# All operations and PSUM banks of an attention-plus-gating kernel in one computed list schedule with hand-placed semaphores, with pair-packed gate, row-tiled value projection and merged output tails

## The chip, the cores and the metric

The kernel runs on one core of one Trainium2 chip. Times are device microseconds of that core. "Span" is the time from the first to the last instruction of the profiled execution; the measured time is some 2 us longer. An execution counts as slow when it is over 1.5% above the fastest of the same kernel; verdicts use the fast ones. On one core the state of a single execution is not always known.

Words used below: PE is the TensorE matmul, PEld its weight load, DVE VectorE, ACT ScalarE, POOL GpSimd. SPq and POOLq are the queues on which the SP and POOL engines issue transfers. The **mode** of a matmul is the part of the array that it uses, rows times columns, as the profile prints it: `128*128` (full), `64*128` (one of two row halves), `128*64` (one of two column halves).

## The reference

Eight batches; each has eight heads of 576 rows of 64 numbers.

```python
def phi(x):                                   # for q and k
    proj = einsum('bhsd,df->bhsf', x, w_phi)  # 64 -> 128
    proj = proj - max(abs(proj), axis=-1)
    return concat([exp(proj), exp(-proj)])    # 256 features
kv  = einsum('bhsf,bhsd->bhfd', phi(k), v)
z   = sum(phi(k), axis=2)
x   = einsum('bhsf,bhfd->bhsd', phi(q), kv) / (einsum('bhsf,bhf->bhs', phi(q), z) + 1e-6)
# x is seen as (8, 576, 512)
gate = sigmoid(causal convolution of x over rows, 5 taps, one weight per channel and tap)
out  = (gate * (x @ w_val)) @ w_out
```

## The kernel before

Per batch it does the K and Q features (PK, PQA: matmul, maximum on DVE, exponentials on ACT), the scaling of v by the maxima (VT, on POOL), the sums KVPS, the numerators and denominators NUM, the transposed x (XT), gate and value (GATE, VAL), and the output. K and Q reach PE transposed: a casting load from DRAM to DRAM on POOL's queue, then a transposing DMA on SP's queue.

```python
    def load_rows(st, src, name, parts):
        b = st.b
        T = qtp.tile([P, H * HALF], BF16, name=name)
        rows = src[b].rearrange("h s d -> h (s d)").rearrange("h (i x) -> i h x", x=256)
        hn = H // parts
        for c in range(parts):
            R = dram.tile([hn * 2 * P, 2 * D], BF16, name=f"{name}R{parts}")
            nc.gpsimd.dma_start(
                R[:, :].rearrange("(h i y) x -> i h (y x)", h=hn, y=2), rows[0:P, c * hn:(c + 1) * hn, :],
            )
            nc.sync.dma_start_transpose(T[:, c * hn * 2 * P:(c + 1) * hn * 2 * P], R[:, :])
        R = dram.tile([H * NT, 2 * D], BF16, name=f"{name}Rt")
        nc.gpsimd.dma_start(
            R[:, :].rearrange("(h i y) x -> i h (y x)", h=H, y=2), rows[P:HALF // 2, :, :],
        )
        nc.sync.dma_start_transpose(T[:, TAIL:H * HALF], R[:, :])
        return T
```

The gate is a convolution, done as ten 128 x 128 matmuls with diagonal weights for each quarter of the channels; the value projection is eight full matmuls:

```python
    def unit_valgate(st, jt):
        XT = st.XT
        GATE = ps2.tile([P, 2, 512], FP32, name="GATE", tag="b")
        for tap in range(5):
            for par in range(2):
                t = par + tap - 4
                i0 = PAD + t // 2
                nc.tensor.matmul(
                    GATE[:, par, 0:HALF], DIAG[:, jt, tap, :], XT[:, jt, t % 2, i0:i0 + HALF],
                    start=(tap == 0), stop=(tap == 4),
                )
        GS = mlp.tile([P, 2, HALF], BF16, name="GS")
        nc.scalar.activation(GS[:, :, :], GATE[:, :, 0:HALF], AF.Tanh)
        VAL = ps2.tile([P, 2, 512], FP32, name="VAL", tag="b")
        for dt in range(4):
            for par in range(2):
                nc.tensor.matmul(
                    VAL[:, par, 0:HALF], WVAL[:, dt, jt * P:(jt + 1) * P],
                    XT[:, dt, par, PAD:PAD + HALF], start=(dt == 0), stop=(dt == 3),
                )
        with nc.allow_low_precision("bf16 gv"):
            nc.vector.scalar_tensor_tensor(
                out=st.GV[jt][:, :, :], in0=GS[:, :, :], scalar=1.0, in1=VAL[:, :, 0:HALF],
                op0=ALU.add, op1=ALU.mult,
            )
```

The order is made by hand: two lists of units are interleaved by weights, and all PSUM tiles are pairs of banks from one pool of four.

```python
... (unit_k, unit_qmax, unit_vscale, unit_qproj, unit_kv, unit_num, unit_xt, unit_out: one function per unit)

    def merge(ua, ub):
        ta, tb = sum(w for w, _ in ua) or 1.0, sum(w for w, _ in ub) or 1.0
        ia = ib = 0
        fa = fb = 0.0
        while ia < len(ua) or ib < len(ub):
            if ib >= len(ub) or (ia < len(ua) and fa <= fb):
                fa += ua[ia][0] / ta
                ua[ia][1]()
                ia += 1
            else:
                fb += ub[ib][0] / tb
                ub[ib][1]()
                ib += 1

    for i in range(B + 1):
        if i + 1 < B:
            load_qk(states[i + 1])
            load_v(states[i + 1])
        if i < B:
            alloc_A(states[i])
            alloc_B(states[i])
        merge(
            units_features(states[i]) if i < B else [],
            units_num(states[i - 1], (2, 3, 4)) + units_mlp(states[i - 1]) if i > 0 else [],
        )
        if i == 0:
            late_constants()
        if i < B:
            merge(units_qproj(states[i]), units_kv(states[i]) + units_num(states[i], (0, 1)))
```

## Time and profile before

| | before |
|---|---|
| measured time, median of 2 | 394.84 us (393.51 to 396.16) |
| span of the profiled execution | 391.9 us |
| PE, DVE, ACT busy | 66%, 44%, 48% of the span |
| one batch in the steady stretch | 40.8 us |

The page of the kernel before: the span, the busy time, and three rows of 40 equal slices (9.8 us each), in which each digit is tenths of busy time, or of full clock.

```profile
span 391.9 us, 6901 instructions
PE 257.9 (66%) x2876; PEld 163.0 (42%) x2876; DVE 171.6 (44%) x253; ACT 186.5 (48%) x261; POOL 142.4 (36%) x207
...
PE   0023387950018895889597958796769856995794
...
PEclk9999998995559898889978996899698969897898
DMA  9994799999997217500742055201600210012003
```

No engine is near its limit, and the row of PE shows a gap of three to four slices after the first fifth. The table of busy time by stretches (start and end in us, length, then each engine's busy us and instructions, the granted PE clock, DMA share, GB/s) gives one steady batch, the gap, and a short stretch inside a batch:

```profile
130.37:170.36 39.99, 31.83 (x359) 20.18 (x360) 21.11 (x31) 22.37 (x30) 13.64 (x20) 0.88 0.36 90
...
79.00:119.00 40.00, 8.65 (x84) 5.21 (x84) 2.76 (x5) 8.40 (x13) 15.03 (x21) 0.62 1.29 193
154.00:160.00 6.00, 5.45 (x61) 3.34 (x60) 0.92 (x2) 1.94 (x2) 1.39 (x2) 0.50 0.92 246
```

In the gap PE works 8.65 of 40 us. The list of waits (who waited for whom: total us, times, longest) names its cause:

```profile
PE KVPS L326 <- ACT OUTs L426: 32.1, 8, 30.7
ACT OUTs L426 <- DMA out_dram<-OUTs: 29.9, 2, 28.2
```

and the timeline of SP's queue in the same stretch shows the store of OUTs behind transposes:

```profile
76.59 8.67 SPq L79 DMA_TRANSPOSE KT<-KTR_1073  x1
...
96.07 8.47 SPq L79 DMA_TRANSPOSE KT<-KTR_1615  x1
104.63 1.00 SPq L432 DMA_DIRECT2D out_dram<-OUTs  x2
```

Each of the large transposes (there are three in this stretch) held the queue for over 8 us (8.67, 8.04 and 8.47), so the store was issued only at 104.6 us, ACT could not reuse its buffer, and PE waited for ACT. In the steady stretch the loss is of another kind: in-order waits along one batch's chain, of which PE's longest, 3.13 us, is for POOL's scaling of v. It comes back at 193.9, 234.6 and 275.5 us, once a batch. Behind it the granted PE clock is 0.50 (the last line of the table above, 154 to 160 us). It is also at half (0.51) from 129.4 to 132.9 us, after 3.5 us in which PE was busy for 1.42. The timeline of PE of before shows both (start, length, instruction, idle time before it and what ended that):

```profile
130.32 2.56 PE L394 MATMUL GATE<-XT,DIAG 128*128 128x288 bf16 x10
...
153.41 0.59 PE L332 MATMUL KVPS<-VTt_1103,KTIL 128*128 128x260 bf16 x2 [3.13 <-POOL VTt_1103 L268]
```

The ten matmuls took 2.56 us; the three groups of ten after them, at full clock, 1.41 each in the same view. (The 1.34 of the prediction is the same length in the view of the critical chain.)

### The profile page before, as it was taken

The page shows a single profiled execution, that of the slowest core. Times are in us where ns is not written, and L with a number is a line of the kernel's source. Part 1 is how long each engine was busy: PE and PEld are TensorE (multiplying, and loading weights), DVE is VectorE, ACT ScalarE, POOL GpSimd, SP SyncE. Part 2 cuts the span into 40 slices and gives each one's busy share as a digit, 9 for nine tenths or more (in the row PEclk, how much of TensorE's full clock was granted, in tenths as well). Part 3 has the DMA queues.
Part 4 walks back from the last instruction along what each step waited for, and adds up shares of the span by engine and source line. Part 5 has one row for each costly group of instructions (what it writes and reads, how often), then busy time and mean ns, then how long its engine had stood idle before and what let it go on. Part 6 is the DMA issues. An engine that isn't in the chain of part 4 may idle for free.

```text
span 391.9 us, 6901 instructions
## 1 busy us (share of the span) xinstructions
PE 257.9 (66%) x2876; PEld 163.0 (42%) x2876; DVE 171.6 (44%) x253; ACT 186.5 (48%) x261; POOL 142.4 (36%) x207
## 2 busy tenths in 40 slices
PE   0023387950018895889597958796769856995794
PEld 0022264620015552655254624562446434643571
DVE  1128046720006672567146723764195517560620
ACT  1117944450027364735564475547355636474522
POOL 8102959786000328022800471045304440426000
PEclk9999998995559898889978996899698969897898
DMA  9994799999997217500742055201600210012003
GB/s 188 172 203 103 124 211 143 187 179 183 184 234 138 46 30 208 122 7 2 204 113 48 2 142 162 63 1 56 188 2 2 72 50 2 2 45 77 2 0 120
DMA packets 85320, 39.31 MB, mean 100 GB/s; under 512 B 44709, under 2 KB 80677, under 8 KB 85290
## 3 DMA queue, kind: packets, MB, share of 16 engines
q1 hardware_dynamic: 65088, 28.32, 31.3%
q0 software_dynamic: 20032, 10.49, 20.1%
q8 instruction: 22, 0.36, 0.4%
q10 hardware_dynamic: 170, 0.08, 0.1%
q14 instruction: 8, 0.07, 0.1%
HBM read 30.48 MB, written 18.87 MB: 126 GB/s over the span
## 4 chain that ended last, share of the span: by engine, by line
PE 38%; DVE 18%; POOL 16%; DMA 10%; SPq 9%; issue 7%; ACT 1%; POOLq 0%; DVEq 0%; ACTq 0%
PE GATE L394 13%; PE VAL L403 9%; DVE XN L361 7%; SPq L79 5%; DMA QTRt<-in_q_dram 4%; DVE MK L214 4%; PE KVPS L326 4%; DMA out_dram<-OUTs 3%; PE KVPS L332 3%; PE PQ L280 3%; DVE XT L380 2%; PE PQ L285 2%; DMA KTR_96<-in_k_dram 2%; SPq L84 2%; SPq L103 2%
## 5 line engine op out<-in xcount | busy, mean ns | idle before, releaser
L219 ACT ACTIVATE KTIL<-PK 128x1024 bf16<-128x1024 f32 (+1 forms) x80 | 70.7, 940 | 72.3 <-DVE MK L214 72.3
L290 ACT ACTIVATE QTIL<-PQ 128x1024 bf16<-128x1024 f32 x64 | 61.6, 1023 | 52.8 <-PE PQ L285 52.8
L245 POOL TENSOR_SCALAR MK<-MK 128x16 f32<-128x16 f32 (+1 forms) x24 | 5.9, 245 | 166.4 <-DVE MK L214 161.0
L338 DVE CAST KVSB<-KVPS 128x520 bf16<-128x520 f32 x16 | 11.2, 700 | 109.9 <-PE KVPS L332 109.9
L394 PE MATMUL GATE<-XT,DIAG 128*128 128x288 bf16 x320 | 51.1, 312 | 1.5 <-DVE XT L382 1.5
L326 PEld LDWEIGHTS <-KTIL 128*128 128x128 bf16 x512 | 28.0, 120 | 50.3 <-issue 45.2
L214 DVE TENSOR_REDUCE MK<-PK 128x8 f32<-128x1024 f32 (+1 forms) x40 | 44.4, 1111 | 9.2 <-PE PK L196 9.0
L403 PE MATMUL VAL<-XT,WVAL 128*128 128x288 bf16 x256 | 42.0, 312 | 0.0
L420 PE MATMUL OUTp<-WOUT,GV 128*128 128x512 bf16 (+1 forms) x160 | 38.5, 380 | 4.0 <-DVE MQB_144 L228 2.3
L399 ACT ACTIVATE GS<-GATE 128x576 bf16<-128x576 f32 x32 | 20.9, 652 | 38.5 <-PE GATE L394 38.5
L394 PEld LDWEIGHTS <-DIAG 128*128 128x128 bf16 x320 | 31.5, 104 | 13.7 <-issue 0.7
L426 ACT ACTIVATE OUTs<-OUTp 128x1024 f32<-128x1024 f32 (+1 forms) x24 | 21.3, 889 | 32.7 <-DMA out_dram<-OUTs 29.9
L408 DVE SCALAR_TENSOR_TENSOR GV<-GS,VAL 128x576 bf16<-128x576 bf16 x32 | 24.1, 752 | 21.2 <-PE VAL L403 21.2
L228 DVE TENSOR_REDUCE MQB_142<-PQA 128x8 bf16<-128x1024 f32 (+1 forms) x20 | 22.2, 1112 | 22.5 <-PE PQA L196 22.5
L403 PEld LDWEIGHTS <-WVAL 128*128 128x128 bf16 x256 | 27.5, 107 | 9.8
L228 DVE TENSOR_REDUCE MQB_144<-PQA 128x8 bf16<-128x1024 f32 (+1 forms) x20 | 22.3, 1113 | 19.6 <-PE PQA L196 19.6
L196 PE MATMUL PK<-W_127,KT 64*128 64x128 bf16 x288 | 16.7, 232 | 19.4 <-DMA KT<-KTR_93 16.7
L375 PE MATMUL XTP<-ident_bf,XN 128*128 128x128 bf16 (+1 forms) x160 | 15.1, 217 | 21.2 <-DVE XN L361 20.8
L361 DVE TENSOR_TENSOR XN<-NUM,RCP 128x512 bf16<-128x512 f32 (+1 forms) x40 | 26.9, 688 | 0.9
L420 PEld LDWEIGHTS <-GV 128*128 128x128 bf16 (+1 forms) x160 | 14.7, 99 | 19.9 <-issue 4.3
L326 PE MATMUL KVPS<-VT_559,KTIL 128*128 128x65 bf16 x32 | 2.2, 219 | 31.1 <-ACT OUTs L426 30.9
L196 PE MATMUL PQA<-W_127,QT 64*128 64x128 bf16 x288 | 15.9, 229 | 9.5 <-DMA QT<-QTR_103 9.0
(226 smaller groups left out, 375.5 us busy)
## 6 DMA issues: line engine op xcount, KB each, us to landing
VN<-in_v_dram SPq DMA_DIRECT2D x16, 512.0 KB, 5.4
out_dram<-OUTs SPq DMA_DIRECT2D x24, 256.0 KB, 2.9
out_dram<-OUTs SPq DMA_DIRECT2D x8, 192.0 KB, 4.3
out_dram<-OUTs SPq DMA_DIRECT2D x8, 128.0 KB, 4.0
KTRt<-in_k_dram POOLq DMA_DIRECT2D x8, 64.0 KB, 11.0
QTRt<-in_q_dram POOLq DMA_DIRECT2D x8, 64.0 KB, 14.5
KTR_165<-in_k_dram POOLq DMA_DIRECT2D x1, 512.0 KB, 11.6
QTR_172<-in_q_dram POOLq DMA_DIRECT2D x1, 512.0 KB, 14.8
```

The source lines that it names most:

```text
L196: nc.tensor.matmul(PS[:, par, x, :], T[ROWS[par], c0:c0 + P], W2[ROWS[par], :], start=True, stop=True,)
L214: nc.vector.tensor_reduce(st.MK[:, 0, s0:s0 + 2 * n].rearrange("p (t x) -> p t x", t=2), PK[:, :, 0:n, :], AX.X, ALU.max, apply_absolute_v ...
L219: nc.scalar.activation(st.KTIL[:, sgn, s0:s0 + 2 * n, :].rearrange("p (t x) f -> p t x f", t=2), PK[:, :, 0:n, :], AF.Exp, scale=1.0 - 2.0 ...
L228: nc.vector.tensor_reduce(st.MQb[:, :].rearrange("p (t s) -> p t s", t=2)[:, :, 4 * u:4 * u + n], PQ[:, :, 0:n, :], AX.X, ALU.max, apply_a ...
L290: nc.scalar.activation(st.QTIL[:, sgn, u, :, :, :], PQ[:, :, :, :], AF.Exp, scale=1.0 - 2.0 * sgn,)
L326: nc.tensor.matmul(KVPS[:, sgn, x * E1:(x + 1) * E1], st.KTIL[:, sgn, s, :], st.VT[sgn][:, s, :], start=(x == 0 and jp == 0), stop=False, ...
L361: nc.vector.tensor_tensor(XN[0:m, :, :].rearrange("p (g x) d -> p g x d", g=2), NUMv[:, :, :, 0:D], RCP[0:m, :, :].unsqueeze(3).to_broadca ...
L394: nc.tensor.matmul(GATE[:, par, 0:HALF], DIAG[:, jt, tap, :], XT[:, jt, t % 2, i0:i0 + HALF], start=(tap == 0), stop=(tap == 4),)
L403: nc.tensor.matmul(VAL[:, par, 0:HALF], WVAL[:, dt, jt * P:(jt + 1) * P], XT[:, dt, par, PAD:PAD + HALF], start=(dt == 0), stop=(dt == 3),)
L408: nc.vector.scalar_tensor_tensor(out=st.GV[jt][:, :, :], in0=GS[:, :, :], scalar=1.0, in1=VAL[:, :, 0:HALF], op0=ALU.add, op1=ALU.mult,)
L420: nc.tensor.matmul(OUTp[0:m, n, :], st.GV[jt][:, :, :].rearrange("p t i -> p (t i)")[:, P * c:P * c + m], WOUT[:, jt, :], start=(jt == 0), ...
L426: nc.scalar.activation(OUTs[0:m, 0:len(cs), :], OUTp[0:m, 0:len(cs), :], AF.Copy)
```

## The change

The intent is to run all engines close to their limits at once. The whole kernel becomes a list of units with a priority, dependencies and a cost; a list scheduler, run when the kernel is built, hands out engines and PSUM banks one by one in the model's time, and its order is emitted with semaphores placed by hand. Besides:
- batch 0's K and Q come by plain loads and are transposed on PE; batches 1 and 2 are loaded at once, at the start;
- GATE: x is kept so that both rows of a pair lie on the partitions, and 12 matmuls of 128 x 64 (six pairs of column halves) do the five taps;
- VAL: 16 matmuls of 64 x 128, in pairs of row halves;
- the row tiles of the Q projection subtract the maxima without a masked copy;
- the last 64 rows of two batches share one output unit; half the padding in the tail of v is gone; single PSUM banks are used where one is enough.

The core of the diff (lines of "..." are cuts):

```diff
--- before.py
+++ after.py
 ...
+DVE_E, DVE_I, DVE_L = 1.0417e-3, 0.065, 0.09
+ACT_E, ACT_I, ACT_L = 0.8333e-3, 0.055, 0.12
+POOL_E, POOL_I, POOL_L = 1.93e-3, 0.06, 0.06
+PE_L = 0.19
+WAKE = 0.045
+DMA_L = 2.0
 ...
+CFG = dict(
+    period=19.0,
+    limit=dict(
+        K=1, QA=1, QF=3, KV=1, NUM=2, XT=2, MQ=1, GATE=1, VAL=1, OUT=2, T0=3,
+    ),
+    off=dict(
+        cast=-28.24, v=-6.0, DG=8.07, K=0.0, Kd=4.34, QA=1.0, QAd=4.0, EK=2.83, VT=1.85, MQ=15.13,
+        QF=19.55, QFd=3.59, KV=21.26, KVd=3.55, NUM=27.88, NUMd=3.0, XT=1.6, GATE=41.98, GATEd=3.0,
+        OUT=55.38, OUTd=1.94, store=0.5,
+    ),
+)
 ...
+    def schedule(self, limit):
 ... (event loop: at each time, each free engine)
 ...
+                    best = None
+                    for o in ready[e]:
+                        if best is not None and (o.prio, o.seq) >= (best.prio, best.seq):
+                            continue
+                        if o.rel > t + 1e-9:
+                            continue
+                        if any(self._from(x, h, e) > t + 1e-9 for x, h in o.deps):
+                            continue
+                        ps = o.ps
+                        if ps is not None and not o.new:
+                            if any(self._from(x, False, e) > t + 1e-9 for x in ps.users):
+                                continue
+                        elif ps is not None:
+                            if live.get(ps.cls, 0) >= limit.get(ps.cls, 9):
+                                continue
+                            if self._place(ps.nb, bank_free, t) is None:
+                                continue
+                        best = o
+                    if best is None:
+                        continue
+                    o = best
+                    again = True
+                    left -= 1
+                    for f in o.opts:
+                        ready[f].remove(o)
+                    o.eng, o.t0 = e, t
+                    o.t1, o.t2 = t + o.occ[e], t + o.vis[e]
+                    if o.dma is not None:
+                        o.t2 = 1e9
+                        heapq.heappush(pend, (o.t1 + 0.6, o.seq, o))
+                        heapq.heappush(times, o.t1 + 0.6)
+                    free[e] = o.t1
 ...
+    def emit(self, tc, nc):
 ... (keeps the planned order; drops waits that an earlier wait implies)
 ...
+                for k, n in need.items():
+                    E.wait_ge(sems[k], n)
+                    for kk, nn in snap[(k, n)].items():
+                        if kn.get(kk, 0) < nn:
+                            kn[kk] = nn
+                out = o.fn(E, None if o.ps is None else o.ps.at)
+                if o.dma is not None:
+                    if o.used or o.key[0] == "out":
+                        s = sem(o.key)
+                        for i in out:
+                            i.then_inc(s, 16)
+                        count[o.key] += 16 * len(out)
+                        o.mark = (o.key, count[o.key])
+                elif o.used:
+                    out[-1].then_inc(sems[o.eng], 1)
+                    count[o.eng] += 1
 ...
+def build(pl, cfg, nc=None, m=None):
 ... (constants)
 ...
+    const("WVa", "POOL", 0.8, lambda E, b: [E.dma_start(
+        m.WV[0:D, :, :], m.w_val.rearrange("(h c) j -> c h j", c=D))], -195, w=["WVa"], dma=3.1, key=("WVa",))
+    const("WVb", "SP", 0.6, lambda E, b: [E.dma_start(m.WV[D:P, :, :], m.WV[0:D, :, :])],
+          -194, r=["WVa"], w=["WVb"], dma=1.5, key=("WVb",))
+    const("WO", "POOL", 0.8, lambda E, b: [E.dma_start(
+        m.WO[:, :, :], m.w_out.rearrange("(jt p) o -> p jt o", p=P))], -194, w=["WO"], dma=3.1, key=("WO",))
 ...
+        if b == 0:
+            for g in range(2):
+                for xi, X in enumerate(("KT", "QT")):
+                    src = (m.k, m.q)[xi][0].rearrange("h s d -> (h s d)").rearrange("(c p x) -> p c x", p=P, x=P)
+                    pl.fresh(("XF", xi, g))
+                    pl.op("xf", "SP", 0.6, lambda E, b_, xi=xi, g=g, src=src: [E.dma_start(
+                        m.XF[:, 18 * xi + 9 * g:18 * xi + 9 * g + 9, :], src[:, 9 * g:9 * g + 9, :])],
+                        -300 + 2 * g + xi, w=[("XF", xi, g)], dma=1.95, key=("XF", xi, g))
+            for g in range(2):
+                for xi, X in enumerate(("KT", "QT")):
+                    for j in range(3):
+                        ps = Banks(1, "T0")
+                        c = 18 * xi + 9 * g + 3 * j
+                        pl.op("T0", "PE", 0.75, lambda E, at, c=c: [E.transpose(
+                            m.PS[:, at, P * y:P * y + P], m.XF[:, c + y, :], m.ident_f[:, :]) for y in range(3)],
+                            -100 + 10 * g + 5 * xi + j, r=[("XF", xi, g), "ident_f"], w=[], ps=ps, new=True)
+                        dst = 1152 * g + 384 * j
+                        pl.op("T0c", ("DVE", "ACT"), {"DVE": dve(384), "ACT": act(384)},
+                              lambda E, at, X=X, dst=dst: [cp(E, m.T[X][0][:, dst:dst + 384], m.PS[:, at, 0:384])],
+                              -99 + 10 * g + 5 * xi + j, w=[(X, 0, g)], ps=ps)
+        else:
+            for g in range(2):
+                for xi, X in enumerate(("KT", "QT")):
+                    src = (m.k, m.q)[xi][b].rearrange("h s d -> (h s d)").rearrange("(c p x) -> c p x", c=2, x=1024)
+                    rk = ("R", xi, g, s)
+                    pl.fresh(rk)
+                    pl.op("cast", "POOL", 0.75, lambda E, at, src=src, xi=xi, g=g: [E.dma_start(
+                        m.R[xi][g][s].rearrange("(p y) x -> p (y x)", y=8), src[g])],
+                        -205 + (10 * b if b > 1 else 0) + 2 * g + xi, w=[rk], dma=1.55,
+                        rel=max(0.0, t0 + off["cast"]), key=("R", xi, g, s))
+                    pl.op("tr", "SP", 1.6, lambda E, at, X=X, xi=xi, g=g: [E.dma_start_transpose(
+                        m.T[X][s][:, 1152 * g:1152 * g + 1152], m.R[xi][g][s][:, :])],
+                        -205 + 10 * b + 2 * g + xi, r=[rk], w=[(X, s, g)], dma=1.8, key=(X, s, g))
 ...
 ... (K and Q features, Q projection, KV, NUM; the whole of batch b in units with a priority)
 ...
+    def mlp(b):
+        s = b % 2
+        t0 = T * b
+        XT = m.XT[s]
+        rx = [("XT", s, y) for y in range(3)] + [("XT0", s)]
+        for jt in range(4):
+            pr = t0 + off["GATE"] + off["GATEd"] * jt
+            gs = ("GS", (4 * b + jt) % 3)
+            pl.fresh(gs, ("GV", s, jt))
+            GS = m.GS[gs[1]]
+            ps = Banks(2, "GATE")
+
+            def mm(E, at, jt=jt):
+                return [E.matmul(
+                    m.PS[ROWS[hh], at + p, 0:HALF], m.DG[:, 2 * jt + hh, 3 * p + dl, :],
+                    XT[:, 2 * jt + hh, dl:dl + HALF], start=(dl == 0), stop=(dl == 2), skip_group_check=True)
+                    for p in range(2) for dl in range(3) for hh in range(2)]
+
+            pl.op("GATE", "PE", 0.76, mm, pr, r=rx + ["DG"], ps=ps, new=True, vis=0.76 + PE_L)
+            pl.op("TANH", "ACT", act(576), lambda E, at, GS=GS: [E.activation(
+                GS[:, :, :], m.PS[:, at:at + 2, 0:HALF], AF.Tanh, scale=0.5)], pr, w=[gs], ps=ps)
+            ps = Banks(2, "VAL")
+
+            def mm(E, at, jt=jt):
+                return [E.matmul(
+                    m.PS[:, at + p, 0:HALF], m.WV[ROWS[p], h, P * jt:P * jt + P], XT[ROWS[p], h, PAD:PAD + HALF],
+                    start=(h == 0), stop=(h == H - 1), skip_group_check=True) for h in range(H) for p in range(2)]
+
+            pl.op("VAL", "PE", 1.0, mm, pr + 0.3, r=rx + ["WVa", "WVb"], ps=ps, new=True, vis=1.0 + PE_L)
+            pl.op("GV", "DVE", dve(576), lambda E, at, jt=jt, GS=GS: [E.scalar_tensor_tensor(
+                out=m.GV[jt][:, s, :, :], in0=GS[:, :, :], scalar=1.0, in1=m.PS[:, at:at + 2, 0:HALF],
+                op0=ALU.add, op1=ALU.mult)], pr + 0.3, r=[gs], w=[("GV", s, jt)], ps=ps)
 ...
 ... (outs: units c = 0..3 for every batch; c = 4, for odd batches, is the tail of two batches)
+            if c < 4:
+                p, j = c % 2, c // 2
+
+                def mm(E, at, p=p, j=j):
+                    return [E.matmul(m.PS[:, at, :], m.GV[jt][:, s, p, P * j:P * j + P], m.WO[:, jt, :],
+                                     start=(jt == 0), stop=(jt == 3)) for jt in range(4)]
+
+                rd = [("GV", s, jt) for jt in range(4)]
+            else:
+                def mm(E, at):
+                    return [E.matmul(m.PS[NT * (2 * y + p):NT * (2 * y + p) + NT, at, :],
+                                     m.GV[jt][:, y, p, 2 * P:HALF], m.WO[:, jt, :], start=(jt == 0), stop=(jt == 3),
+                                     skip_group_check=True)
+                            for jt in range(4) for y in range(2) for p in range(2)]
+
+                rd = [("GV", y, jt) for jt in range(4) for y in range(2)]
+            pl.op("OUT", "PE", 0.88, mm, pr, r=rd + ["WO"], ps=ps, new=True, vis=0.88 + PE_L)
+            pl.op("OUTc", ("ACT", "DVE"), {"ACT": act(512), "DVE": dve(512)},
 ...
 ... (the old body, pools and merge() are removed)
 ...
+    pl = Plan()
+    build(pl, CFG, nc, m)
+    pl.schedule(CFG["limit"])
+    with nc.allow_low_precision("bf16 operands"):
+        pl.emit(tc, nc)
```

## The prediction

> **What bounds it now.** No engine. In the table of busy time by stretches, one steady batch (from its first GATE matmul to the next batch's, 130.4 to 372.7 us) takes about 40.8 us; PE is busy 32 of it, DVE 21, ACT 22, POOL 13.6, and the DMA share is 0.1 to 0.36. The time is in-order waiting: in the chain of waits, each batch goes Kmax, OUT issue, POOL scaling of v (5.8 us), KVPS, normalisation, GATE/VAL. While PE waits 3.1 us for the POOL tail of v, DVE idles 7 us and the granted clock falls to 0.50 (154 to 160 us); the next ten GATE matmuls take 2.56 us instead of 1.34. [...] There are two one-off losses: first PE work at 16.7 us and first GATE at 64 us (transposed loads), and a stall from 79 to 119 us, PE busy 9 of 40, where a store of OUTs sits on the SP queue behind transposes of 8 to 9 us each (list of waits: 28.2 us ACT on that store, 30.7 us PE on ACT). It costs some 25 us.
>
> **Work after the change, per batch**, from measured durations (1024-wide exp 0.94 us back to back; 1024-wide max 1.13; 512-wide DVE 0.6; 512-wide POOL 1.04; 288-column matmul 0.122; 512-column 0.215; 65-column about 0.03):
> - PE: features 2.6, Q projection 2.1, KV 2.3, NUM 2.2, transposes 1.1, GATE 3.0 (was 4.9: six column-tiled pairs for ten), VAL 4.0 (same: row pairs), OUT 4.0 (was 4.3): about 21.3 us warm, against 25.
> - DVE 19, ACT 19, plus 2.4 of output copies that either may take: about 20.3 each.
> - POOL 12.5 (v tail halved) plus 3 of issue. DMA the same bytes, 4.7 MB, in longer pieces: my estimate 20 us, from transposes of 512 KB in 4 us [...].
> Row pairs are seen in this trace: two 64-row 512-column matmuls advance together at 0.22 us a pair. Column pairs are not[...].
>
> **Critical path.** Removed work is only some 4 us of PE a batch. The gain is overlap: three to four batches interleaved, single banks handed out one by one, so the period falls from 40.8 to near the fullest engine. Floors are 20 to 21 on PE, ACT, DVE and DMA at once; I expect 85 to 92% packing: period 23 to 25 us. The 79-119 stall should go. The first batch comes by plain loads and PE transposes: first K matmul at 7 to 9 us, first GATE near 45.
> Sum: PE does little before 45 us (15 of its 170 us); 155 us at 90% is 172; tail 9; about 226, plus about 3 from span to measured time: **230 us**, range **213 to 252**.
> Chances: faster by over 2% 0.97, within 2% 0.02, slower 0.01.
>
> **Signs.** PE busy above 75% of the span, DVE and ACT about 70%, granted clock near 1.0 after the ramp; GATE groups of 12 in about 0.76 us (1.4 if column pairs don't overlap); no wait over 5 us after the ramp; GATE starts of successive batches 22 to 26 us apart; DMA share 0.7 to 1.
>
> **What would make it wrong.** The order is fixed by a cost table: where loads land later than planned (DMA is nearly full, the SP queue is in order), every engine waits in its order: 27 to 30 us a batch, 250 to 270. Column tiles that don't overlap add 3 us a batch. [...] The other way, 95% packing gives about 215.

Four passages that rested on no trace are cut from it: what was said to lower the clock, a figure for column pairs, a figure for loads of v, and what a change of tiling mode may do. The sum came to 45 + 172 + 9 = 226 us of span, 230 us in measured time, and no term of it is cut. Two figures under it were not shown when they were put. GATE's 3.0 us a batch is an estimate: 24 pairs at the measured 0.122 us of one 288-column matmul, if column pairs advance together. The 20 us of DMA a batch, one of the floors but no term of the sum, is an estimate too: in the trace of before, six of the eleven transposes of 512 KB landed in 4.0 to 4.6 us (the longest in 17.0), and loads of v of 512 KB in 4.0 to 12.3 us, 5.4 in the median. That the clock was 0.50 and ten GATE matmuls took 2.56 us is measured.

## The result, and the profile after

| | before | after |
|---|---|---|
| measured time, median | 394.84 us | 258.81 us (258.60, 259.01) |
| ratio of the fast runs | | 0.6547 (95% interval 0.6484 to 0.661) |
| span | 391.9 us | 256.8 us |
| PE, DVE, ACT busy | 66%, 44%, 48% | 81%, 71%, 68% |

Ratios here and below are the mean time of one kernel's fast runs over that of the other's from the same rounds, so they are not quite the ratio of the medians quoted. The time fell by 34 to 35%, but it lies above the range of 213 to 252 us.

The page after, the same lines:

```profile
span 256.8 us, 8459 instructions
PE 206.9 (81%) x3693; PEld 144.7 (56%) x3708; DVE 181.5 (71%) x277; ACT 174.6 (68%) x240; POOL 119.1 (46%) x203
...
PE   0260838487968999899899999998998999999960
...
PEclk9999977897999999999999999999999999999997
DMA  6999999999535999789999993960170013103041
```

The gap is gone and so are the long waits of PE; but the first quarter of the span is still thin. Busy time by stretches (columns as before), from the first GATE to the end of PE's work, cut at the three merged output tails and so two batches to a line in the middle:

```profile
62.00:115.40 53.40, 48.04 (x902) 32.89 (x909) 44.52 (x65) 43.78 (x60) 28.66 (x49) 0.99 0.87 166
115.40:165.20 49.80, 47.60 (x910) 32.89 (x914) 42.63 (x64) 43.15 (x61) 26.75 (x45) 1.00 0.92 196
165.20:214.80 49.60, 47.15 (x911) 33.16 (x918) 43.27 (x64) 42.96 (x61) 23.50 (x39) 1.00 0.29 90
214.80:249.00 34.20, 32.60 (x497) 20.96 (x495) 19.17 (x33) 13.13 (x20) 4.45 (x7) 1.00 0.19 67
sum 187.00, PE 175.40 PEld 119.90 DVE 149.59 ACT 143.02 POOL 83.36; mean PE 43.85 PEld 29.97 DVE 37.40 ACT 35.76 POOL 20.84
```

PE is busy 175.4 of 187.0 us there (94%), at full clock: after the first GATE this kernel is bound by PE. One batch takes 24.8 us (49.6 / 2), inside the predicted 23 to 25. The predicted sum of three terms, beside what came of each:

| term | predicted | measured |
|---|---|---|
| ramp, to the first GATE | 45 us | 62.0 us |
| body, from there to the end of PE's work | 155 us of PE work at 90%, 172 us | 175.4 us of PE work at 94%, 187.0 us |
| tail | 9 us | 7.8 us |
| span | 226 us | 256.8 us |

So two terms of about equal size are missing: 17 us in the ramp and 15 us in the body.

**A clue for the body.** The timeline of PE after, in a dense stretch. Here the start of one group to the start of the next is read, for the length in the second column runs past the start of the next group (1.16 us in the first pair below, 1.09 from start to start):

```profile
181.67 1.16 PE L787 MATMUL PS<-XT,WV 64*128 64x288 bf16 x16
182.76 0.62 PE L720 MATMUL PS<-ident_bf,XN 128*128 128x128 bf16 x8
...
198.78 1.17 PE L787 MATMUL PS<-XT,WV 64*128 64x288 bf16 x16
199.79 0.38 PE L612 MATMUL PS<-QT,W 64*128 64x512 bf16 x2
```

The same VAL group (16 matmuls, mode 64*128) takes 1.09 us when the next group is in another mode (first pair), and 1.01 us when the next group is in its own (second pair). It is so for every kind of group that was followed by both. Between 115.4 and 214.8 us (four batches) the medians in the trace are, from start to start:

| group | next in the same mode | next in another mode | difference |
|---|---|---|---|
| K features, 8 matmuls of 64*128 | 0.235 us | 0.328 us | 0.093 us |
| end of KV, 2 of 128*128 | 0.117 us | 0.208 us | 0.091 us |
| NUM, 16 of 128*128 | 0.498 us | 0.590 us | 0.092 us |
| VAL, 16 of 64*128 | 0.996 us | 1.094 us | 0.098 us |
| GATE, 12 of 128*64 | never | 0.860 us | |

There are 104 such changes in these four batches, 26 a batch, and 191 from the first GATE to the end. At some 0.095 us each that is 18 us. The plan's cost table has 1.0 us for VAL and 0.76 for GATE: right for the work, with nothing for a change. (15 of the kernel's 3,708 matmuls, all of OUT, are missing from this trace. In e10_later, with the same order of PE and none missing, PE is busy 177.2 of 187.8 us after the first GATE, again 94%.)

**A clue for the ramp.** List of waits after, the line for PE on a transfer, and SP's queue from the start:

```profile
PE PS L428 <- DMA QTIL<-in_k_dram: 12.7, 2, 6.6
```

```profile
0.94 0.47 SPq L420 DMA_DIRECT2D QTIL<-in_k_dram  x1
1.47 0.61 SPq L420 DMA_DIRECT2D QTIL<-in_q_dram  x1
2.13 1.57 SPq L420 DMA_DIRECT2D QTIL<-in_k_dram  x1
3.74 9.52 SPq L420 DMA_DIRECT2D QTIL<-in_q_dram  x1
13.30 12.21 SPq L449 DMA_DIRECT2D VN<-in_v_dram  x2
```

(QTIL is where batch 0's plain loads are put for a while.) The issue of the fourth plain load began at 3.7 us and held the queue for 9.5 us; the four landed at 6.0, 16.2, 26.3 and 28.2 us. In that time POOL's queue had eight casting loads (batches 1 and 2) and the two weight loads under way, issued between 1.5 and 8.5 us. The trace's records of DMA packets from 2 to 26 us:

| what | packets | bytes in one | mean time of one | share of the 16 engines |
|---|---|---|---|---|
| casting loads, POOL's queue | 128 | 18,432 | 1,377 ns | 0.46 |
| weights, POOL's queue | 1,024 | 1,024 | 96 ns | 0.26 |
| plain loads of K and Q, SP's queue | 3,940 | 512 | 31 ns | 0.32 |

So the loads that the ramp waits for got a third of the DMA engines.

### The profile page after: what moved, and what is told of

Its sections match the earlier page's. It is cut to its first block, busy times and chain, and to the rows that moved or that the text cites. A ratio compares the mean times of both kernels' runs of the same rounds, so it can differ in the third digit from the quotient of the medians.

```text
span 256.8 us, 8459 instructions
## 1 busy us (share of the span) xinstructions
PE 206.9 (81%) x3693; PEld 144.7 (56%) x3708; DVE 181.5 (71%) x277; ACT 174.6 (68%) x240; POOL 119.1 (46%) x203
## 3 DMA queue, kind: packets, MB, share of 16 engines
q0 software_dynamic: 1952, 9.31, 20.2%
## 4 chain that ended last, share of the span: by engine, by line
PE 59%; DVE 16%; ACT 11%; DMA 9%; issue 2%; SPq 0%; DVEq 0%
PE PS L787 11%; PE PS L813 10%; DMA QTIL<-in_k_dram 9%; PE PS L776 9%; PE PS L665 7%; ACT QTIL L625 6%; DVE MQb L586 5%; PE PS L701 4%; ACT KTIL L500 3%; DVE MK L495 3%; PE PS L612 3%; PE PS L720 2%; PE PS L490 2%; PE PS L618 2%; DVE GV L792 2%
## 5 line engine op out<-in xcount | busy, mean ns | idle before, releaser
L537 POOL TENSOR_TENSOR VT<-VN,EK 128x512 bf16<-128x512 f32 x64 | 65.7, 1045 | 18.8 <-ACT EK L528 18.7
L625 ACT ACTIVATE QTIL<-PS 128x1024 bf16<-128x1024 f32 x64 | 61.9, 1036 | 12.6 <-PE PS L618 12.6
L500 ACT ACTIVATE KTIL<-PS 128x1024 bf16<-128x1024 f32 x64 | 62.5, 1032 | 6.4 <-PE PS L490 4.3
L586 DVE TENSOR_REDUCE MQb<-PS 128x8 bf16<-128x1024 f32 (+1 forms) x40 | 44.1, 1113 | 3.1 <-PE PS L574 2.6
L495 DVE TENSOR_REDUCE MK<-PS 128x8 f32<-128x1024 f32 x32 | 39.0, 1219 | 4.6 <-PE PS L490 2.7
L792 DVE SCALAR_TENSOR_TENSOR GV<-GS,PS 128x576 bf16<-128x576 bf16 x32 | 24.1, 753 | 18.8 <-PE PS L787 14.6
L787 PE MATMUL PS<-XT,WV 64*128 64x288 bf16 x512 | 37.1, 283 | 0.1
L776 PE MATMUL PS<-XT,DG 128*64 128x288 bf16 x384 | 30.1, 292 | 2.4 <-ACT QTIL L625 1.4
L813 PE MATMUL PS<-WO,GV 128*128 128x512 bf16 x113 | 28.3, 379 | 2.9 <-DVE GV L792 1.1
L787 PEld LDWEIGHTS PS<-XT,WV 64*128 64x128 bf16 x512 | 22.9, 94 | 8.8 <-issue 1.6
L665 PE MATMUL PS<-VT,KTIL 128*128 128x65 bf16 x512 | 22.6, 202 | 2.2 <-ACT QTIL L625 1.3
L665 PEld LDWEIGHTS PS<-VT,KTIL 128*128 128x128 bf16 x512 | 20.2, 103 | 5.1 <-issue 4.3
L428 PE MATMUL PS<-ident_f,QTIL 128*128 128x128 f32 x36 | 8.7, 425 | 14.2 <-DMA QTIL<-in_k_dram 12.7
```

The lines of the kernel that those rows point to most:

```text
L495: pl.op("Kmax", "DVE", dve(1024), lambda E, at, u=u: [E.tensor_reduce(MK[:, 0, 8 * u:8 * u + 8].rearrange("p (t x) -> p t x", t=2), m.PS[: ...
L500: pl.op("Kexp", "ACT", act(1024), lambda E, at, u=u, g=g: [E.activation(KTIL[:, g, u, :, :, :], m.PS[:, at:at + 2, :].rearrange("p t (x f) ...
L537: pl.op("VT", "POOL", pool(512), lambda E, at, u=u, hh=hh, a=a, g=g, EK=EK: [E.tensor_tensor(m.VT[s][:, g, u, :, :, 0:D], m.VN[s][:, 4 * h ...
L586: pl.op("Qmax", "DVE", dve(256 * nx), lambda E, at, u=u, nx=nx: [E.tensor_reduce(MQb[:, :].rearrange("p (t s) -> p t s", t=2)[:, :, 4 * u: ...
L625: pl.op("Qexp", "ACT", act(1024), lambda E, at, u=u, g=g: [E.activation(m.QTIL[s][:, g, u, :, :, :], m.PS[:, at:at + 2, :].rearrange("p t ...
L665: res.append(E.matmul(m.PS[:, at + sg, x * E1:(x + 1) * E1], m.KTIL[s][:, sg, 2 * g + a, par, x, :], m.VT[s][:, sg, 2 * g + a, par, x, :], ...
```

## The experiments

Twelve runs; each has runs of the kernel before on the same chip. Unless said otherwise each is the changed kernel with one edit, gave the right result, and lists four executions. The medians quoted take in all four, slow ones too; the ratios are of the fast ones alone.

### a0_after: the changed kernel again

Expected:

> The changed kernel unchanged, as the base for the other runs of this call. Both theories: 257 to 260 us, first GATE matmul near 62 us, and 24.8 us from one batch to the next in the steady stretch.

Measured: 259.41 us (258.45 to 259.61), ratio to before 0.6581. First GATE at 61.5 us; from the second to the third merged output tail (two batches) 49.5 us. It is the base for what follows: ramp 61.5, body 188.2 (to the end of PE's work), span 257.5 us.

### Changes of mode, added and paid for: e2_switch and e3_same

A one-column matmul in the middle of KV, NUM and GATE groups, once in another mode, once in the group's own. For GATE:

```diff
-                return [E.matmul(m.PS[ROWS[hh], at + p, 0:HALF], m.DG[...], XT[...], ...)
-                    for p in range(2) for dl in range(3) for hh in range(2)]
+                for p in range(2):
+                    if p == 1:   # e2_switch: 64 rows, 128 columns
+                        res.append(E.matmul(m.PS[:, at + p, 0:1], m.W2[ROWS[0], :], m.W2[ROWS[0], 0:1], ...))
+                                 # e3_same: 128 rows, 64 columns
+                        res.append(E.matmul(m.PS[ROWS[0], at + p, 0:1], m.ident_bf[:, 0:D], m.ident_bf[:, 0:1], ...))
+                    res += [... the six matmuls of this p, as before]
```

> One extra one-column matmul with 64 rows in the middle of each KV group, and of each four-head NUM and GATE group (80 in all, 160 more changes of the tiling mode); what it writes is overwritten by the next matmul, so the result stays right. Order and all else as in the changed kernel. Theory (each change of tiling mode costs PE about 0.095 us that the plan leaves out, and PE is the limit in the steady stretch): 160 x 0.095 = 15 us of PE time, of which 11 to 16 us is seen beyond the run with the same extra matmuls without a change of mode; 270 to 280 us. Rival (PE has slack in the steady stretch, which is paced by late loads or by DVE and ACT): within 4 us of that run.

> The same 80 extra one-column matmuls in the mode of the group that they stand in: the control for the run before. Theory: 80 x 0.03 to 0.06 us, so 1 to 5 us slower than the changed kernel. Rival: under 1 us slower.

Measured: e2_switch 273.82 us (272.87 to 274.20), ratio 0.6949; e3_same 260.39 us (260.20 to 260.89), ratio 0.6613. The extra matmuls alone cost 0.98 us over a0_after, on the border between theory and rival of e3_same; the 160 extra changes cost 13.4 us more, as expected. Not all of it is in the body: the first GATE comes 2.9 us later in e2_switch (14 of the changes lie before it, and the mean clock there was 0.85 against 0.91). After the first GATE, 146 extra changes made PE's busy time 12.1 us longer, 0.083 us each, and the kernel 10.0 us, 0.069 us each, since PE's idle time fell by 2.0 us. The timeline of PE in e2_switch around one GATE group:

```profile
180.06 0.56 PE L787 MATMUL PS<-XT,DG 128*64 128x288 bf16 x6 [0.47 <-DVE GV L804]
180.55 0.17 PE L786 MATMUL PS<-W 64*128 64x1 bf16 x1
180.65 0.56 PE L787 MATMUL PS<-XT,DG 128*64 128x288 bf16 x6
```

and in e3_same:

```profile
169.25 0.56 PE L787 MATMUL PS<-XT,DG 128*64 128x288 bf16 x6
169.65 0.17 PE L786 MATMUL PS<-ident_bf 128*64 128x1 bf16 x1
169.65 0.56 PE L787 MATMUL PS<-XT,DG 128*64 128x288 bf16 x6
```

From the first half of GATE to the second is 0.59 us with two changes and 0.40 without: 0.095 us a change. That changes cost PE time, and that most of this PE time is the kernel's time, is shown.

### Loads taken out of the body: e5_noload

```diff
+    gone = {o for o in pl.order if o.name in ("cast", "tr", "v", "vt") and o.seq >= pl.second}
+    pl.order = [o for o in pl.order if o not in gone]   # no loads from batch 2 on; and no waits on them
```

> Wrong result on purpose: from batch 2 on nothing is loaded; K, Q and v of batches 0 and 1 are used again, and every other instruction and its order is the same. Theory (in the steady stretch PE is the limit, with its changes of mode): the two batches between the second and the third merged output tail still take 48.4 to 50 us (49.6 in the changed kernel); the time falls only in the ramp, to 250 to 258. Rival (late loads pace the steady stretch): that interval falls under 47 us and the time under 247.

Measured: 251.62 us (251.53 to 252.07), ratio 0.6377; wrong result. The two batches between the second and the third tail took 49.5 us, exactly as with the loads, and from the first GATE to the end of PE's work it took 188.0 us (a0_after 188.2). Late loads don't pace the body: that rival fell. Of the 7.8 us that it was faster, 5.9 came from the ramp: the fourth plain load landed at 22.7 us instead of 28.1, and the first GATE started at 55.5 us instead of 61.5. Another 1.5 us came from the tail after PE's last matmul (6.3 us instead of 7.8).

### The plan told of the cost: e6_cost

```diff
+MODE = dict(K="row", QF="row", QA="row", VAL="row", Kt="row32", NUMt="col", XTt="col", GATE="col")
+TURN, KEEP = 0.095, 0.0
...
-                    o.t1, o.t2 = t + o.occ[e], t + o.vis[e]
+                    turn = TURN if e == "PE" and MODE.get(o.name, "full") != mode else 0.0
+                    o.t1, o.t2 = t + o.occ[e] + turn, t + o.vis[e] + turn
```

> The plan is told the cost of a change of tiling mode (0.095 us of PE when the next PE unit is in another mode) and draws up its order with that; nothing else differs. Theory (PE work is what it is; the plan's order already fits): within 3 us of the changed kernel, so 256 to 262 us. Rival (the body is long because the order was drawn up for a faster PE than there is): 3 to 8 us faster, 251 to 256 us.

Measured: 264.07, 268.62, 260.58 and 268.41 us; two of the four were slow. In the profiled execution (fast) the first GATE was at 63.1 us and the body took 191.3 us, with 194 changes of mode instead of 191 and 15.4 us of idle PE instead of 11.6. The rival (a better-informed order is faster by 3 to 8 us) fell; of the two fast executions one (260.58) lay in the expected 256 to 262 and one above it. In this run, knowing the cost didn't help: the priorities left as many changes as before. Why its executions spread by 8 us was not followed up.

### Holding back the loads of the ramp: e1_hold, e4_hold2, e7_hold3

Three attempts at the ramp, with the order of PE, ACT and DVE kept. First, all ten transfers on POOL's queue wait for the plain loads:

```diff
+    held = [o for o in pl.order if o.name in ("WVa", "WO") or o.name == "cast" and o.seq < pl.third]
+    last = [o for o in pl.order if o.name == "xf"][-1]
+    for o in held:
+        o.deps.append((last, True))
```

> The eight casting loads of batches 1 and 2 and the two weight loads wait until the last of the four plain loads of batch 0 has landed; every other order is the same. Theory (the first loads share the DMA engines with twelve other transfers): the last of the four plain loads lands at 13 to 16 us instead of 28, the first GATE starts at 49 to 54 us instead of 62, and the time falls by 8 to 12 us, to 247 to 251. Rival (the ramp is long because the chain of work of one batch is long and PE runs at half clock there): the loads land earlier but the first GATE moves by less than 3 us and the time by less than 3 us.

(The text says twelve transfers in its theory, and so does the next; there are ten.) Measured: 254.45 us (253.29 to 257.55, the last one slow), ratio 0.6451. (The half clock of the rival, here and in the three expectations like it below, is in the traces: in the ramp of the changed kernel it was 0.50 from 35.6 to 42.3, 49.2 to 52.5 and 59.5 to 62.8 us, and 1.00 up to 35.5 us.) The plain loads landed at 5.8, 8.1, 10.0 and 12.0 us, better than expected, but the first GATE started at 58.0 us and the time fell by 5 us: between the theory and the rival. The gain was given back to a new wait. PE's fixed order puts batch 1's K before the rest of batch 0, and batch 1's first two transposes, now beside batch 2's casts and the weights, took 22.6 and 22.3 us from issue to landing, and PE waited 4.2 us for the first.

Second, batch 2's casts are moved behind batch 0's scaling of v as well:

> As the run that held twelve loads back, but the four casting loads of batch 2 stand after batch 0's scaling of v on the POOL queue, just ahead of batch 3's first one, so that they no longer run beside batch 1's transposes; batch 1's casts and the two weight loads follow batch 0's plain loads as before. Theory (that run gave its gain back because batch 1's transposes, beside casts and weights, took 22 us instead of 4 to 7, and PE's fixed order puts batch 1's K ahead of batch 0's remaining work): batch 1's first transpose lands by 26 us instead of 39, the first GATE starts at 50 to 54 us, and the time is 246 to 251. Rival (from there on the ramp is the chain of work and the halved clock): first GATE at 57 to 59 us and 253 to 255 us, as in that run.

Measured: 269.25, 250.87, 251.28 and 269.32 us: two fast and two slow executions, and the profile fell in a slow one. The two fast ones lie where the theory put them (246 to 251, or just above); the ratio of the fast ones is 0.6361. The slow profile says how the collision looks, though it may not explain a difference between kernels: from 38 to 56 us the casts' packets of 18,432 bytes took 3,498 ns on average (1,377 in the table above) and the transposes' packets of 256 bytes 198 ns (28 in the changed kernel from 44 to 60 us). The medians did not move (1,376 and 18 ns), so some packets took very long, not all of them a little longer. The question needed another edit.

Third, one after the other, by waits: the weights wait for batch 1's third transpose, batch 2's casts for the fourth:

> The loads of the ramp one after the other, every other order kept: batch 1's casts wait for batch 0's plain loads, the two weight loads for batch 1's third transpose, batch 2's casts for batch 1's fourth transpose. Theory (in the ramp the casting loads, whose packets of 18,432 bytes hold a DMA engine for 1.4 to 3.5 us each, starve the plain loads and the transposes on the other queue, whose packets have 256 to 1,024 bytes): transposes of batch 1 land within 4 to 7 us each, first GATE at 50 to 54 us, all four executions within 1% of each other, 247 to 252 us. Rival (the ramp's length is the chain of work and the halved clock; which load runs first only shuffles it): first GATE at 57 to 61 us, 253 to 258 us.

Measured: 256.41 us (255.40 to 257.83), ratio 0.6504, first GATE at 59.1 us: a miss, in the rival's range. Batch 1's first three transposes (0.29 MB each), with few other transfers beside them, did land 3.5 to 6.5 us after issue. The list of waits shows why this doesn't speak for the rival:

```profile
PE PS L665 <- POOL VT L543: 8.3, 1, 8.3
POOL R L441 <- DMA QT<-R: 7.9, 1, 7.9
```

POOL issues the casts and also scales v, in order. While it waited 7.9 us for the transpose before it could issue a load, batch 1's v stood behind, and PE waited 8.3 us for that (L665 is KV). The edit had put a wait for a transfer in front of work.

### Loads that are not needed yet stand behind: e10_later

```diff
     held = [... the four casts of batch 1, WVa, WO ...]          # wait for batch 0's plain loads
+    late = [o for o in pl.order if o.name == "cast" and pl.second <= o.seq < pl.third]   # batch 2
+    next_ = [o for o in pl.order if o.name == "cast" and o.seq > pl.third][:2]           # batch 3
+    for o in late:
+        o.deps.append((turned, True))          # batch 1's fourth transpose
+    # both are put behind batch 1's first scaling of v on POOL
```

> As the run whose executions spread from 251 to 269 us, but the loads of batches 2 and 3 that are not yet needed (six casts) stand behind batch 1's first scaling of v on POOL, and batch 2's casts wait for batch 1's fourth transpose, so that POOL is not blocked and no cast runs beside batch 1's transposes. PE, ACT and DVE keep their order. Theory (the ramp is as long as the DMA engines need for what stands ahead of batch 0's GATE, and loads that are needed later were in front of it): first GATE at 49 to 54 us, 247 to 252 us, executions within 1.5% of each other. Rival (chain of work and halved clock): first GATE at 57 us or later, 254 us or more.

Measured: 249.26 us (248.53, 248.57, 249.95; and one slow, 253.58), ratio 0.6336. In a fast profile the plain loads landed at 5.7, 8.3, 9.9 and 11.9 us, and the first GATE started at 51.2 us instead of 61.5. SP's queue, to be read beside the one above, and the first GATE:

```profile
4.17 1.87 SPq L420 DMA_DIRECT2D QTIL<-in_q_dram  x1
6.08 2.98 SPq L449 DMA_DIRECT2D VN<-in_v_dram  x2
...
16.61 2.10 SPq L445 DMA_TRANSPOSE KT<-R  x1
...
51.18 1.00 PE L776 MATMUL PS<-XT,DG 128*64 128x288 bf16 x10
```

The body was left as it was: 187.8 us (a0_after 188.2). So 10.3 us of the ramp were transfers standing in front of what was needed first: the casts of batch 1 and the weights in front of batch 0, and the casts of batch 2 in front of batch 1; the rival, that the chain of work sets the ramp, fell for that part. The spread among executions was 2%, not within the 1.5% expected.

### Is it the bytes or the packets? e8_short

```diff
-    src = (m.k, m.q)[xi][b].rearrange("h s d -> (h s d)").rearrange("(c p x) -> c p x", c=2, x=1024)
+    src = (m.k, m.q)[xi][b].rearrange("h s d -> (h s d)").rearrange("(c a p x) -> c p a x", c=2, a=8, x=256)
-    m.R[xi][g][s].rearrange("(p y) x -> p (y x)", y=8), src[g]
+    m.R[xi][g][s].rearrange("(a p y) x -> p a (y x)", a=8, y=2), src[g]
```

> The changed kernel with one edit: the casting loads run through the same bytes in pieces of 256 numbers (512 bytes written, 1 KB read) rather than in one run of 8 rows, so that their packets are short, as in the kernel before. Nothing is held back. Theory (long packets of the cast queue starve the other queue): in the ramp the fourth plain load lands earlier than 28 us, at 18 to 24, although all the same bytes are under way; the time may go either way, since the casts themselves get slower: 252 to 264 us. Rival (the plain loads are late because of the bytes beside them, whatever their packets): the fourth plain load lands at 27 to 30 us.

Measured: 258.65 us (257.51 to 259.27 fast, one slow at 263.81), ratio 0.6536. With the same bytes under way, the fourth plain load landed at 20.2 us instead of 28.1 and the third at 14.0 instead of 26.2. The page's line for POOL's queue, after and in e8_short, shows the edit: the same megabytes in twelve times the packets.

```profile
q0 software_dynamic: 1952, 9.31, 20.2%
```

```profile
q0 software_dynamic: 23008, 9.33, 29.8%
```

From 2 to 26 us the casts' packets had 512 bytes and took 59 ns, and SP's queue got a share of 0.54 of the DMA engines for its plain loads of K, Q and v. With long packets SP's queue had had 0.32 of the engines in that stretch (the table above). So the rival (the bytes beside them, whatever their packets; 27 to 30 us) fell; how an engine shares its time among queues is not in the records. (The short casts also took POOL longer to issue, until 12.0 us instead of 9.0, which may be a small part of it.) But the casts then cost more engine time (29.8% of the span for 20.2%) and batch 1's transposes landed 12 to 14 us after issue. The first GATE came at 58.3 us, 3 us earlier than in a0_after, but the body took 192.8 us, and the time was not clearly different.

### Fewer changes of mode: e11_order and e9_fewer

The order is drawn up anew: the plan knows the 0.095 us, prefers a unit in the mode at hand when it is at most 1.6 us less urgent, and its offsets and limits were searched again under that model. By trace, 171 changes of mode in all instead of 217, and 141 instead of 191 after the first GATE.

```diff
+TURN, KEEP = 0.095, 1.585
-                        if best is not None and (o.prio, o.seq) >= (best.prio, best.seq):
+                        key = o.prio + (KEEP if e == "PE" and MODE.get(o.name, "full") != mode else 0.0)
+                        if best is not None and (key, o.seq) >= (best_key, best.seq):
 ... (CFG: new offsets and limits)
```

e11_order is this alone, with the loads as they were; e9_fewer has it together with the waits of e7_hold3 (the place of batch 2's casts follows a slightly wider rule).

> Only the new order (the one of 163 changes of mode among PE's units instead of 204), with the loads of the changed kernel left as they are. Theory (changes of mode are PE time, and PE is the limit after the ramp): 41 x 0.095 = 4 us less than the changed kernel after the first GATE, whatever the ramp does; from first GATE to last matmul 181 to 186 us instead of 187 to 188, in all 252 to 258 us. Rival (the new order gains only through the ramp): 187 us or more from the first GATE to the last matmul.

> The run above with the loads one after the other, and an order drawn up anew: the plan is told the 0.095 us of a change of mode, prefers a PE unit in the mode at hand when it is at most 1.6 us less urgent, and its offsets and limits are searched again; 163 changes of mode among PE's units instead of 204. Theory (changes of mode are PE time, and PE is the limit): 41 x 0.095 = 4 us less than that run, if the new order costs nothing elsewhere; a range of 0 to 6 us less. Rival (changes of mode cost nothing that matters): no faster than that run.

Measured: e11_order 255.52 us (255.16 to 257.73), ratio 0.6508: first GATE at 61.4 us, as in a0_after, and 184.9 us from there to the end of PE's work instead of 188.2. That is 3.3 us for 50 changes saved there (0.095 each would be 4.8). The new offsets could also have gained by less waiting. Against e7_hold3, which has the old order and, like e11_order, no matmul missing from its trace and the same clock after the first GATE (0.99), PE's busy time there fell from 178.2 to 175.5 us and its idle time only from 9.8 to 9.4: most of the gain is busy time, though less than 50 changes at 0.095 us would give. e9_fewer 247.04 us (246.62 to 248.45), ratio 0.627: first GATE at 52.2 us, body 184.9 us, span 244.8 us. It was 9.4 us faster than e7_hold3, more than the 0 to 6 expected: in the new order batch 1's fourth transpose was issued at 23.3 us, ahead of the weights, and landed at 26.9 (in e7_hold3 at 27.3, behind them, and 39.5). So POOL's wait for it no longer held batch 1's v, and the ramp gained as well, by 6.9 us. e9_fewer is faster than both kernels given, by 37% and by 5% (0.627 / 0.6581 = 0.953, on two chips).

## Why the prediction was right or wrong

**Right.** No engine bounded the kernel before, and the gain was overlap: the batch fell from 40.8 to 24.8 us, inside 23 to 25. The gap from 79 to 119 us went. PE is the fullest engine at 81% of the span, DVE 71%, ACT 68%, the clock is full after the ramp (0.99 to 1.00), and the DMA share is 0.87 to 0.92 as long as there are loads. Column pairs overlap: 12 GATE matmuls and a change take 0.86 us; without the overlap their columns alone would take 12 x 0.122 = 1.46. The packing looks better than put (94% instead of 90%), but these 94% have the changes of mode in them: 155 us of work in 187.0 are 83%.

**Wrong, the body.** The failed step is the term "155 us at 90% is 172", which has as its sum of PE work "about 21.3 us warm" a batch. The sum has every matmul at its measured rate and nothing between them. In the two middle lines of the table PE was busy 47.60 and 47.15 us for two batches, 23.7 us each. 26 changes of mode a batch, at 0.083 to 0.095 us of PE time, are 2.2 to 2.5 us a batch: the difference. For the 191 after the first GATE that is 16 to 18 us of PE work. 155 + 18 = 173, and PE was busy 175.4 us. The 155 was right: counted by the trace, with each kind of matmul at its rate within its own mode (an estimate from the first column of the table by group and its like), the matmuls after the first GATE are about 155 us of work. (PE's 31.5 us of busy time before it, where 15 were put, therefore took nothing out of the body.) The prediction named changes of tiling mode at its end as a risk without a size, and did not price them. The trace of before had the size in it: K features of 8 matmuls take, from start to start, 0.33 us before another mode and 0.23 before their own.

**Wrong, the ramp.** The failed step is "first GATE near 45". Loads were counted per batch in the steady stretch ("my estimate 20 us"), as if batch 0 could have the DMA engines to itself. But the plan starts the loads of batches 1 and 2 and the weights at once, and from 2 to 26 us these had a share of 0.72 of the engines, against 0.32 for the plain loads. The first K matmul came at 14.2 us instead of 7 to 9. Putting behind what was not needed yet gave 10.3 of the 17 us (e10_later). It took three attempts, for each hold moved the wait: to batch 1's transposes, then to POOL's work on v. What remains, from 51.2 to 45 us, is open: PE's clock is at 0.55 to 0.84 of full from 20 to 50 us in that run, and the chain of one batch is long, but no run parts the two.

**The listed danger.** The prediction gave "250 to 270 us" for the case that loads land late and every engine waits in its order. The number fell inside, but by luck: it was to come from 27 to 30 us a batch, and the batch took 24.8. Late loads did it in the ramp, and in the body not at all (e5_noload).

## What to carry to other kernels

A kernel that packs many small tiled matmuls should count its changes of tiling mode and price them like matmuls; with PE as the limit, each was time here (0.069 us of the kernel for each of the 146 added after the first GATE), and an order with fewer of them was faster (ratio to before 0.6508 with 171 in e11_order, 0.6581 with 217 in a0_after; the new offsets may have a part in it). In a ramp, list every transfer that is issued ahead of the first work and ask which of them is not yet needed: here loads of the next two batches, in packets of 18,432 bytes on another queue, delayed the load that the chip was waiting for (it landed at 28.1 us beside them, at 20.2 with the same bytes in packets of 512, at 11.9 with them held back). Where an engine both issues loads and computes in order, a wait put on a load stands in front of its work (7.9 us on POOL in e7_hold3, 8.3 us on PE behind it), so move the load behind the work instead of making it wait.
